# Layer 1 of a Strassen expert stage with tokens on the partitions: 512 moving columns, the gate in the relu, h turned by two DMAs a unit

## The chip, the cores and the metric

The kernel runs on one core of a Trainium2 chip. The metric is the device time of one execution in microseconds, taken as the median of several runs. Beside it stands one profiled execution, whose span (first to last instruction) all views of the profile divide up. The engines are PE (TensorE, with its weight loads as PEld), DVE (VectorE), ACT (ScalarE), POOL (GpSimd) and SP (SyncE, which here only issues DMAs).

## The reference

Attention with a sliding window of 128 and ALiBi bias on 8 batches, 8 heads, 576 positions and head size 64 gives x, 4608 tokens of 512 features. A dense mixture of 8 experts follows, with gates from a Sinkhorn iteration:

```python
logits = x @ w_gate
P = np.exp(logits - logits.max())
for _ in range(8):
    P /= P.sum(1, keepdims=True) + 1e-09
    P /= P.sum(0, keepdims=True) + 1e-09
    P *= N / E
for e in range(E):                     # E = 8, F = 1024, D = 512
    h = np.maximum(x @ w1[e], 0.0)
    out += P[:, e:e + 1] * (h @ w2[e])
```

Every token goes through every expert. P is positive, so P * relu(x @ w1) is relu((P x) @ w1) and also relu scaled after the fact.

## The kernel before

Attention comes first, batch by batch. Experts 0 and 1 are computed in the gaps of attention and of the gate iteration by a "filler": a list of small pieces (layer 1 with 512 token columns, layer 2 with 512 output columns) from which the program takes as many as the moment holds. Their results go to DRAM (ysp); x itself goes there too (xd).

From about 320 us on runs the stage that the change is about: experts 2 to 7 by Strassen's method in Winograd's form. The tokens are taken in 18 groups of 256 (two blocks of 128), and a **unit** is one group with one expert, 108 in all, in the order of the list `units`. Only the units of experts 6 and 7 in the first group use ordinary layer 1 matmuls (`l1_bank`), and the last unit an ordinary layer 2 (`plain`).

Layer 1 of a unit. x (scaled by the gate) lies in xset with the features on the partitions, cut into four quarters B11 to B22 and four sums T1 to T4 that DVE makes (`sums_x`, L947). Seven **parts** (`part`, L1014), named a11, s1, s2, a12, s3, s4, a22 after the quarter or sum of W1 that they use, are multiplied. Each part is four row blocks times two halves of the contraction: eight matmuls with a 128x128 block of W1 as stationary operand and 128 token columns moving. The hidden features come out on the partitions. The products are added up in three banks A, B and C of PSUM with the help of copies: after a11 ACT copies A to B; after s1 it copies C to s5; after s2 it copies B to C. a12 is then added to A and relu gives slot 0 of h; s3 is added to B, DVE adds s5 (below: **p+**) and relu gives slot 3; s4 is added to C, DVE adds s5 (**c+**) and relu gives slot 1; a22 is added to B and relu gives slot 2. Each of these waits is a hand-over between PE, ACT and DVE.

Layer 2 of a unit runs one unit later, between the parts of the next. Its left operands are the slots of h and the sums that DVE makes of them at the start of the next unit (`make_sums`, L1035: three operations, of 1024, 1024 and 512 columns). Seven **products** (`product`, L1048) of four matmuls each, a 128x128 block of h as stationary operand and 256 columns of W2 or a sum of its quarters moving, are added up in PSUM over the six experts of a group. At a group's end DVE gathers the seven sums into acc (`gather`), adds the results of experts 0 and 1 (`begin`), and the rows are stored (`finish`).

What feeds a unit. ACT multiplies the group's two x tiles by the gate (`scale_x`, L923, two operations a unit, for the unit after next); SP then turns each by a transposing DMA of 128x512 (`turn_xs`, L935). The tokens are reloaded once a group (L918, on SP's queue), as are the results of experts 0 and 1 (`load_y`, L1066, on SP's queue) and the stores (`finish`, on SP's queue). W1 and W2 sums of the experts (`quads_w1`, `sums_of`) are DVE work too, taken from a list by `some` in the first units (`more_sums`, L1156).

All orders are written out by hand: the program text is the order in each engine's queue (the loop at L1163), and waits come from the data alone. PSUM has four banks for the parts (tag pmm) and four for the sums of the products.

Of the kernel before, what the change touches and what calls it, by code (L numbers as in the profile page):

```python
# [14 lines left out]
def kernel(  # L15
# [89 lines left out]
    def unit_atoms(e, b0, nb, pool, tag, bufs, finish):  # L105
# [5 lines left out]
        halves = 2 if e == 0 and b0 < RI else 1  # L111
# [140 lines left out]
    if True:  # L252
# [314 lines left out]
        first_y: list = []  # L567

        def keep(e, blk, ps):
            if blk < RI and e == 0:  # L570
                if not first_y:
                    first_y.append(per.tile([P, RI, HD], FP16, name="y_first", tag="a8", bufs=8))
                nc.vector.tensor_copy(out=first_y[0][:, blk, :], in_=ps)
                if blk == RI - 1:
                    nc.sync.dma_start(out=ysp[0, 0:RI].rearrange("m p d -> p m d"), in_=first_y[0])
                return
            store(2)
# [324 lines left out]
        N = len(units)  # L902
        HF = Fd // 2
        h: dict = {}
        Ms: dict = {}
# [4 lines left out]
        xtok = [acc.rearrange("p m d -> p (m d)").bitcast(FP16)[:, HD * i : HD * i + HD] for i in range(2)]  # L910
        xs = [xset[i // 2][:, 4 + 2 * (i % 2) : 6 + 2 * (i % 2), :].rearrange("p q n -> p (q n)") for i in range(4)]

        def strassen(n):
            return n >= E - 2 or units[n][1] < E - 2

        def load_x(g):
            for m in range(2):
                nc.sync.dma_start(out=xtok[m], in_=xd[2 * g + m])  # L918

        load_x(groups[0])  # L920
        balance(7)

        def scale_x(n):  # L923
            if n >= N:
                return
            g, e = units[n]
            for m in range(2):
                blk = 2 * g + m
                nc.scalar.mul(out=xs[2 * (n % 2) + m], in_=xtok[m], mul=P_sb[:, blk, e : e + 1])  # L929
            if e == E - 1 and n + 1 < N:  # L930
                if g == groups[0]:
                    xtok[:] = [per.tile([P, HD], FP16, name=f"xtok_{i}", tag="yo", bufs=YO) for i in range(2)]
                load_x(units[n + 1][0])

        def turn_xs(n):  # L935
            if n >= N:
                return
            for m in range(2):
                nc.sync.dma_start(
                    out=xset[n % 2][:, 2 * m : 2 * m + 2, :].rearrange("p q (d t) -> p (q d) t", t=P),  # L940
                    in_=xs[2 * (n % 2) + m],
                    transpose=True,
                )
# [3 lines left out]
        def sums_x(n):  # L947
            if n >= N or not strassen(n):
                return
            x = xset[n % 2]  # L950
# [4 lines left out]
        def quads_w1(e):  # L955
# [5 lines left out]
            elif e == E - 1:  # L961
                t = per.tile([P, 2, 2, HF], FP16, name=f"s_{e}", tag="xT", bufs=4)
                q.update(s1=t[:, 0], s2=t[:, 1])
                q["s3"] = [per.tile([P, HF], FP16, name=f"s3_{k}", tag="yo", bufs=YO) for k in range(2)]
# [5 lines left out]
            def one(to, a, b, op):  # L970
                if isinstance(q[to], list):
                    for k in range(2):
                        nc.vector.tensor_tensor(out=q[to][k], in0=q[a][:, k], in1=q[b][:, k], op=op)
# [13 lines left out]
        def new_h(n):  # L987
            h[n] = per.tile([P, 8, NF2, P], FP16, name=f"hs_{n}", tag="hT", bufs=2)

        def l1_bank(n, i):  # L990
            g, e = units[n]
            if i == 0:
                new_h(n)
            x = xset[n % 2][:, 0:4].rearrange("p q (d t) -> p (q d) t", t=P).rearrange("p (b d) t -> p d b t", b=2)
            ps = aps.tile([P, 2, HB], FP32, name=f"psh_{n}_{i}", tag="pmm", bufs=4)
            for f in range(2):
                ft = 2 * i + f
                for dt in range(NDT):
                    nc.tensor.matmul(  # L999
                        out=ps[:, f, :],  # L1000
                        lhsT=W1L[e][:, dt, P * ft : P * ft + P],
                        rhs=x[:, dt],
                        start=(f == 0 and dt == 0),
                        stop=(dt == NDT - 1),
                        skip_group_check=True,
                    )
            fh, j = 2 * (i // 2), 2 * (i % 2)
            nc.scalar.activation(
                out=h[n][:, fh : fh + 2, j : j + 2, :].rearrange("p t f k -> p f t k"),
                in_=ps.rearrange("p f (t k) -> p f t k", t=2),  # L1010
                func=AF.Relu,
            )

        def part(n, ps, w, x, start=False):  # L1014

            q = SL[units[n][1]][w]
            q = q if isinstance(q, list) else [q[:, k] for k in range(2)]
            for j in range(NF2):
                for k in range(2):
                    nc.tensor.matmul(  # L1020
                        out=ps[:, j, :],
                        lhsT=q[k][:, P * j : P * j + P],
                        rhs=xset[n % 2][:, x, P * k : P * k + P],
                        start=(start and j == 0 and k == 0),
                        stop=(k == 1),
                        skip_group_check=True,
                    )

        def bank(n, name):
            return aps.tile([P, NF2, P], FP32, name=f"ps{name}_{n}", tag="pmm", bufs=4)  # L1030

        def relu(n, slot, src):
            nc.scalar.activation(out=h[n][:, slot], in_=src, func=AF.Relu)  # L1033

        def make_sums(n):  # L1035
            t = h[n]
            nc.vector.tensor_tensor(out=t[:, 4:6], in0=t[:, 0:2], in1=t[:, 2:4], op=ALU.add)  # L1037
            nc.vector.tensor_tensor(out=t[:, 6:8], in0=t[:, 1:4:2], in1=t[:, 0:3:2], op=ALU.subtract)
            nc.vector.tensor_tensor(out=t[:, 1], in0=t[:, 0], in1=t[:, 3], op=ALU.add)

        LEFT = {3: 0, 4: 3, 5: 4, 2: 5, 6: 6, 7: 7, 1: 1}
        RIGHT = {1: "f1", 2: "q11", 3: "f3", 4: "f4", 5: "q22", 6: "f6", 7: "f7"}
        BANK = {3: (0, 0), 4: (0, 1), 5: (1, 0), 2: (1, 1), 6: (2, 0), 7: (2, 1), 1: (3, 0)}

        def ends(n):
            return n >= 0 and units[n][1] == (E - 2 if units[n][0] == groups[-1] else E - 1)

        def product(n, *which):  # L1048
            if n < 0:
                return  # L1050
            g, e = units[n]
            for m in which:
                bk, half = BANK[m]
                if bk not in Ms:
                    Ms[bk] = mps.tile([P, 2, 2 * P], FP32, name=f"psM_{bk}")
                for f in range(NF2):
                    nc.tensor.matmul(  # L1057
                        out=Ms[bk][:, half, :],
                        lhsT=h[n][:, LEFT[m], f, :],
                        rhs=W2L[e][RIGHT[m]][:, f, :],  # L1060
                        start=(e == 2 and f == 0 and half == 0),
                        stop=(ends(n) and f == NF2 - 1 and (half == 1 or m == 1)),
                        skip_group_check=True,
                    )
# [17 lines left out]
        def gather(g, *which):  # L1082
            q4 = acc.rearrange("p m (c n) -> p (m c) n", c=2)
            for m in which:
                bk, half = BANK[m]
                ps = Ms[bk][:, half, :]
                for lo, step, op in {
                    1: ((0, 3, ALU.add),),
                    2: ((2, 0, ALU.add), (3, 0, ALU.subtract)),
                    3: ((1, 2, ALU.add),),  # L1090
                    4: ((0, 2, ALU.subtract),),
                    5: ((0, 0, ALU.subtract), (1, 0, ALU.add)),
                    6: ((3, 0, ALU.add),),
                    7: ((0, 0, ALU.subtract),),
                }[m]:
                    if step:
                        a = q4[:, lo : lo + step + 1 : step, :]
                        p2 = ps.unsqueeze(1).to_broadcast([P, 2, HB])
                    else:
                        a, p2 = q4[:, lo, :], ps  # L1100
                    nc.vector.tensor_tensor(out=a, in0=a, in1=p2, op=op)  # L1101
# [184 lines left out]
```

## Time and profile before

| what | us |
|---|---|
| median of 3 runs (1001.0 to 1003.34) | 1001.36 |
| the profiled execution | 1001.61 |
| its span | 999.8 |
| 340 to 980 us: PE busy of 640 | 639.92 |
| 340 to 980 us: DVE busy of 640 | 512.60 |
| 340 to 980 us: ACT busy of 640 | 528.83 |
| landing of the 212 turns of x, median | 2.5 |

The chain of waits is followed back from the last instruction; each step says which engine's work released the next. Its granted TensorE clock is 1.0 throughout. In a group's row stand the tile written and the tile read, the shape, the count, the busy time and the mean duration of one in ns. A matmul's duration is longer than the pitch at which matmuls follow each other, since they are pipelined; the pitch is read from the start times. A DMA's landing is counted from its issue.

### The profile page before, as it was taken

How to read it: one execution, taken by the hardware profiler on the slowest of the kernel's cores; microseconds unless marked ns; L12 is line 12 of the kernel's file. 1: busy time of each engine (PE TensorE's matmuls, PEld its weight loads, DVE VectorE, ACT ScalarE, POOL GpSimd, SP SyncE). 2: the span in 40 equal slices, each digit the busy share in tenths (PEclk: the TensorE clock that was granted, in tenths of full speed). 3: DMA queues.
4: the chain of work that ended last, by engine and by line, in shares of the span. 5: the costliest groups of instructions: out<-in, count | busy, mean ns of one | idle time of the engine just before them, and what ended most of it. 6: DMA issues, size and time to landing. Idle time of an engine off the chain costs nothing.

```text
span 999.8 us, 28277 instructions
## 1 busy us (share of the span) xinstructions
PE 988.3 (99%) x11731; PEld 816.0 (82%) x11731; DVE 762.0 (76%) x1593; ACT 718.0 (72%) x1216; POOL 110.0 (11%) x202
## 2 busy tenths in 40 slices
PE   7999999999999999999999999999999999999998
PEld 5645665566545899999999999999999999999997
DVE  5737677665688989887887787787787787787787
ACT  7655545554435768888888888888888888888885
POOL 3314444354110000000000000000000000000000
PEclk9999999999999999999999999999999999999999
DMA  9998999989997324333333433333433433333371
GB/s 250 212 271 218 187 233 230 234 170 183 222 201 152 81 54 97 82 61 94 86 56 95 86 76 75 88 73 75 96 76 65 99 78 65 96 76 66 96 116 49
DMA packets 264978, 123.08 MB, mean 123 GB/s; under 512 B 204433, under 2 KB 255633, under 8 KB 264849
## 3 DMA queue, kind: packets, MB, share of 16 engines
q1 hardware_dynamic: 249152, 100.65, 45.4%
q0 software_dynamic: 15264, 20.46, 11.5%
q8 instruction: 92, 1.51, 0.6%
q14 instruction: 38, 0.30, 0.1%
q10 hardware_dynamic: 432, 0.16, 0.1%
HBM read 78.30 MB, written 23.59 MB: 102 GB/s over the span
## 4 chain that ended last, share of the span: by engine, by line
PE 91%; DVE 5%; ACT 2%; DMA 1%; issue 1%; DVEq 0%; ACTq 0%
PE psM L1057 31%; PE psB L1020 14%; PE psy L159 11%; PE psA L1020 9%; PE psC L1020 9%; PE psh L137 9%; PE psh L118 3%; PE psS L457 1%; PE psN L491 1%; DVE pt L468 1%; DMA k<-in_k_dram 1%; ACT pt L463 1%; PE psh L999 1%; DMA xset<-xs 1%; DVE xsb L502 1%
## 5 line engine op out<-in xcount | busy, mean ns | idle before, releaser
L1057 PEld LDWEIGHTS <-hs 128*128 128x128 f16 x2996 | 271.0, 98 | 22.4 <-DVE hs L1037 0.4
L1057 PE MATMUL psM<-w2l,hs 128*128 128x256 f16 x1440 | 186.6, 273 | 0.2 <-DVE hs L1037 0.2
L1020 PEld LDWEIGHTS <-w1l 128*128 128x128 f16 x2848 | 181.4, 98 | 4.8 <-issue 0.4
L1033 ACT ACTIVATE hs<-hs 128x512 f16<-128x512 f16 x212 | 130.4, 629 | 36.2 <-DVE hs L1203 26.6
L1203 DVE TENSOR_TENSOR hs<-psB,s5y 128x512 f16<-128x512 f32 x106 | 73.3, 692 | 97.9 <-ACT xs L929 92.2
L1020 PEld LDWEIGHTS <-s 128*128 128x128 f16 x2136 | 141.6, 98 | 6.7 <-issue 0.2
L929 ACT ACTIVATE xs<-xtok,L_sb 128x512 f16<-128x512 f16 x204 | 135.8, 720 | 2.1 <-DMA xset<-xs 2.1
L159 PE MATMUL psy<-w2t,hT 128*128 128x512 f16 x576 | 135.3, 379 | 0.0
L1057 PE MATMUL psM<-more,hs 128*128 128x256 f16 x864 | 129.5, 273 | 0.0
L1020 PE MATMUL psB<-xset,s 128*128 128x128 f16 x1424 | 108.5, 219 | 0.1
L1020 PE MATMUL psA<-xset,w1l 128*128 128x128 f16 x1424 | 108.5, 219 | 0.0
L149 ACT ACTIVATE hT<-psh 128x512 f16<-128x512 f32 (+1 forms) x104 | 60.1, 581 | 63.5 <-PE psh L137 63.4
L159 PEld LDWEIGHTS <-hT 128*128 128x128 f16 x576 | 54.0, 98 | 58.2 <-issue 1.1
L463 ACT ACTIVATE pt<-psS 128x1024 f16<-128x1024 f32 x64 | 64.6, 1022 | 50.4 <-PE psS L457 49.9
L137 PE MATMUL psh<-xT,w1t 128*128 128x512 f16 (+1 forms) x448 | 99.0, 364 | 0.0
L1037 DVE TENSOR_TENSOR hs<-hs 128x1024 f16<-128x1024 f16 x107 | 73.9, 691 | 20.6 <-ACT hs L1033 18.6
L1194 ACT COPY psC<-psB 128x512 f32<-128x512 f32 x106 | 60.4, 570 | 38.6 <-PE psB L1020 38.6
L579 DVE CAST yo<-psy 128x512 f16<-128x512 f32 x65 | 44.6, 690 | 50.8 <-PE psy L159 50.1
L1186 ACT COPY s5y<-psC 128x512 f32<-128x512 f32 x106 | 62.2, 587 | 22.4 <-PE psC L1020 22.4
L615 POOL DMA_DIRECT2D w2t<-in_moe_w_dram x2 | 1.8, 882 | 669.0 <-PE psA L1020 661.0
L468 DVE TENSOR_TENSOR pt<-pt,mask 128x1024 f16<-128x1024 f16 x64 | 53.6, 837 | 28.3 <-ACT pt L463 28.1
L1101 DVE TENSOR_TENSOR acc<-acc,psM 128x256 f32<-128x256 f32 (+1 forms) x162 | 73.9, 503 | 0.3
(131 smaller groups left out, 1548.8 us busy)
## 6 DMA issues: line engine op xcount, KB each, us to landing
s5y<-ysp SPq DMA_DIRECT2D x36, 256.0 KB, 3.0
ysp<-yo SPq DMA_DIRECT2D x65, 128.0 KB, 4.4
v<-in_v_dram SPq DMA_DIRECT2D x32, 256.0 KB, 4.6
out_dram<-acc SPq DMA_DIRECT2D x31, 256.0 KB, 2.5
q<-in_q_dram SPq DMA_DIRECT2D x5, 1024.0 KB, 6.4
k<-in_k_dram SPq DMA_DIRECT2D x5, 1024.0 KB, 9.2
xtok<-xd SPq DMA_DIRECT2D x34, 128.0 KB, 2.3
w2t<-in_moe_w_dram POOLq DMA_DIRECT2D x4, 1024.0 KB, 12.3
```

What stands on the lines that cost most here:

```text
L137: nc.tensor.matmul(out=ps[:, 0:nt], lhsT=w1ts[e][:, dt, P * ft : P * ft + P], rhs=xT[:, at : at + nb, dt, :], start=(dt == 0), stop=(dt == ...
L159: nc.tensor.matmul(out=ps, lhsT=st["hT"][:, ft, P * ms : P * ms + P], rhs=w2ts[e][:, ft, :], start=(ft == 0), stop=(ft == NFT - 1),)
L463: nc.scalar.activation(out=pt, in_=ps.rearrange("p a y n -> p (a y) n"), func=AF.Exp, scale=scale)
L468: nc.vector.tensor_tensor(out=pt, in0=pt, in1=mask_of[kb][:, 4 * u : 4 * u + 4, :], op=ALU.mult)
L929: nc.scalar.mul(out=xs[2 * (n % 2) + m], in_=xtok[m], mul=P_sb[:, blk, e : e + 1])
L1020: nc.tensor.matmul(out=ps[:, j, :], lhsT=q[k][:, P * j : P * j + P], rhs=xset[n % 2][:, x, P * k : P * k + P], start=(start and j == 0 and ...
L1033: nc.scalar.activation(out=h[n][:, slot], in_=src, func=AF.Relu)
L1037: nc.vector.tensor_tensor(out=t[:, 4:6], in0=t[:, 0:2], in1=t[:, 2:4], op=ALU.add)
L1057: nc.tensor.matmul(out=Ms[bk][:, half, :], lhsT=h[n][:, LEFT[m], f, :], rhs=W2L[e][RIGHT[m]][:, f, :], start=(e == 2 and f == 0 and half = ...
L1101: nc.vector.tensor_tensor(out=a, in0=a, in1=p2, op=op)
L1186: nc.scalar.copy(out=s5, in_=pc)
L1203: nc.vector.tensor_tensor(out=h[n][:, 3], in0=pb, in1=s5, op=ALU.add)
```

## The change

Layer 1 of the stage is turned round: the x blocks become the stationary operand (two weight loads of 128x128 a part) and W1 moves, 512 columns at a time, so a part is two matmuls and the tokens come out on the partitions.

```diff
-        def part(n, ps, w, x, start=False):
-            for j in range(NF2):
-                for k in range(2):
-                    nc.tensor.matmul(
-                        out=ps[:, j, :],
-                        lhsT=q[k][:, P * j : P * j + P],
-                        rhs=xset[n % 2][:, x, P * k : P * k + P],
...
+        def part(n, name, w, x, start=False):
+            for k in range(2):
+                nc.tensor.matmul(
+                    out=psum(name),
+                    lhsT=xset[n // NE % 2][:, x, P * k : P * k + P],
+                    rhs=q[k],
...
```

x is no longer scaled: the gate, now one number per partition, is the scale of the relu. So x is turned and its sums are made once a group (`turn_x2`, `sums_x`, tokens XT0, XT1, SX), not once a unit. The relu writes hr, and h reaches the layout of layer 2 by two transposing DMAs of 128x1024 a unit, on SP's queue: the first after slots 0 and 3, the second after slots 1 and 2.

```diff
+        def relu(n, slot, src):
+            blk = 2 * g + slot % 2
+            nc.scalar.activation(out=hr[:, AT[slot]], in_=src, func=AF.Relu, scale=P_sb[:, blk, e : e + 1])
+
+        def turn_h(n, i):
...
+            nc.sync.dma_start(
+                out=hs[n % 2][:, 2 * i : 2 * i + 2].rearrange("p s f k -> p (s f) k"),
+                in_=hr[:, 2 * i : 2 * i + 2].rearrange("p s f -> p (s f)"),
+                transpose=True,
             )
+        def add_h(n, slot, name):
+            to = hr[:, AT[slot]]
+            nc.vector.tensor_tensor(out=to, in0=psum(name), in1=s5, op=ALU.add)
+            relu(n, slot, to)
+            if slot == 3:
+                turn_h(n, 0)
```

hr is one buffer, hs is two. The sums of h become five operations of 512 columns (`sum_h`, tokens t1, t4, t5, t6, t7). The products come in the order 3, 4, 2, 6, 1, 5, 7 from one stream over all units, and run one unit and four products behind: a unit does the last four of the unit before last and the first three (3, 4 and 2; the last of them needs t5) of the one before. Their sums rotate over five banks, four as before and one of pmm's; A, B and C are the other three. The order of a unit is a string of tokens, X being a product, W one weight sum, F a piece of the filler, g a gather:

```diff
+        plans = (
+            "a11 X s1 X s2 a12 X s3 p+ s4 c+ t5 X t6 t7 X X t4 a22 X t1",
+            "a11 g4 X s1 X g3 s2 g6 X g5 a12 s3 p+ s4 X c+ X X a22 t5 g7 t6 X t4 t1 t7 Y0 XL0",
+            "a11 g2 s1 X g1 FIN X s2 a12 X s3 p+ s4 X c+ X t5 t4 a22 XT0 t6 X X t7 t1 XL1",
+            "a11 X s1 X s2 a12 X s3 p+ s4 c+ X X t5 t6 a22 X XT1 t4 t1 t7 X B0 Y1",
+            "a11 X s1 X s2 a12 X s3 s4 p+ X c+ t5 X a22 X t4 t6 t1 X SX t7",
+            "a11 s1 X X s2 a12 X s3 s4 p+ X c+ X t5 t4 t6 a22 t7 t1 X X B1",
+        )
+        first = {
+            0: "a11 s1 W W F s2 a12 F W W s3 p+ s4 c+ F W W a22 F",
+            1: "a11 s1 F s2 a12 F s3 p+ s4 c+ t5 t6 X t1 X t4 a22 X t7 Y0",
+            4: "L0 X X L3 X X L1 t5 X t6 t4 X L2 X SX t7 t1",
+            5: "L0 X X L3 X X L1 t5 X t6 t4 X L2 X B1 t7 t1",
+            N - 1: "a11 s1 X B1 s2 X a12 X s3 p+ s4 X c+ t5 X t6 X a22 X t1 t4 g3 X t7 X g4 X g2 X g6 g1 g5 g7",
+        }
+        sums_at = {1: 3, 2: 3, 3: 2, 4: 4, 5: 3, 6: 3, 9: 4, 10: 3}
```

The loads of x (XL) and of experts 0 and 1 (Y) and the stores (FIN) move from SP's to POOL's queue; x has one token tile, so its second load waits until the first turn has read it:

```diff
         def load_y(g, e):
-            nc.sync.dma_start(out=y, in_=ysp[e, 2 * g : 2 * g + 2].rearrange("m p d -> p m d"))
+            nc.gpsimd.dma_start(out=y, in_=ysp[e, 2 * g : 2 * g + 2].rearrange("m p d -> p m d"))
...
-                    nc.sync.dma_start(out=out[t0 : t0 + P, :], in_=a)
+                    nc.gpsimd.dma_start(out=out[t0 : t0 + P, :], in_=a)
...
+                elif tok in ("XL0", "XL1"):
+                    if gi + 1 < len(groups):
+                        nc.gpsimd.dma_start(out=xst[int(tok[2])], in_=xd[2 * groups[gi + 1] + int(tok[2])])
```

Expert 7's weights are loaded earlier, within the gate iteration, as soon as expert 0's last result is kept; three of its W1 sums lie in six tiles of another tag. Its W2 is reloaded for the last unit in eight pieces over four units, not in one piece. The last block of expert 1 has layer 2 pieces of half the size, and six of them (not three whole ones) are left for the stage's first units. The two halves of the last unit's layer 2 start with the features whose transpose comes first.

```diff
         for it in range(7):
             balance(it)
-        aux = per.tile([P, 4, NF2, HB], FP16, name="aux", tag="w2t", bufs=2)
+            if first_done and E - 1 not in W1L:
+                load_last(E - 1)
...
-        while filler.l1 or filler.todo or len(filler.l2) > 3:
+        while filler.l1 or filler.todo or len(filler.l2) > 6:
...
-            if n == N - E + 2:
-                load_w2(E - 1)
+            if N - NE + 1 <= n < N - 1:
+                for i in range(2):
+                    load_w2(E - 1, 2 * (n - N + NE - 1) + i, 8)
```

More of the change, by code (lines that the diff above doesn't have):

```diff
@@ L109, in unit_atoms @@
         st: dict = {}
-        halves = 2 if e == 0 and b0 < RI else 1
+        halves = 2 if (e == 0 and b0 < RI) or (e == 1 and b0 == NBLK - 4) else 1
         def l1_pair(ft):
@@ L576, in keep @@
                 return
+            if e == 0 and blk == NBLK - 1:
+                first_done.append(blk)
             store(2)
@@ L1029, in bank @@
[L1029 to L1048, printed above, removed]
+        pp: dict = {}
+        def psum(name):
+            if name not in pp:
+                pp[name] = aps.tile([P, GT], FP32, name=f"ps{name}", tag="pmm", bufs=4)
+            return pp[name]
@@ new lines, in part @@
+        def part(n, name, w, x, start=False):
+            g, e = units[n]
+            q = SL[e][w]
+            q = q if isinstance(q, list) else [q[:, k] for k in range(2)]
+            for k in range(2):
[3 more added lines that the diff above has]
+                    rhs=q[k],
+                    start=(start and k == 0),
+                    stop=(k == 1),
+                    skip_group_check=True,
+                )
@@ new lines, in plain_l1 @@
+        def plain_l1(n, slot, name):
+            g, e = units[n]
+            m, fh = slot % 2, slot // 2
+            for dt in range(NDT):
+                nc.tensor.matmul(
+                    out=psum(name),
+                    lhsT=xset[n // NE % 2][:, 2 * m + dt // 2, P * (dt % 2) : P * (dt % 2) + P],
+                    rhs=W1L[e][:, dt, HF * fh : HF * fh + HF],
+                    start=(dt == 0),
+                    stop=(dt == NDT - 1),
+                )
+            relu(n, slot, psum(name))
@@ L1049, in product, with sum_h @@
+        def add_h(n, slot, name):
[4 more added lines that the diff above has]
+                turn_h(n, 0)
+        def sum_h(n, to):
             if n < 0:
                 return
-            g, e = units[n]
[L1052 to L1064, printed above, removed]
+            t = hs[n % 2]
+            x, y, op = {
+                5: (1, 3, ALU.add),
+                6: (1, 0, ALU.subtract),
+                1: (0, 3, ALU.add),
+                4: (0, 2, ALU.add),
+                7: (3, 2, ALU.subtract),
+            }[to]
+            nc.vector.tensor_tensor(out=t[:, AT.get(to, to)], in0=t[:, AT[x]], in1=t[:, AT[y]], op=op)
@@ new lines, in ends, with product @@
+        def ends(n):
+            return units[n][1] == (E - 2 if units[n][0] == groups[-1] else E - 1)
+        stream = [(n, m) for n in range(N - 1) for m in ORDER]
+        def product():
+            n, m = stream.pop(0)
+            g, e = units[n]
+            half = BANK[m][1]
+            ps = sum_of(g, m)
+            for f in range(NF2):
+                nc.tensor.matmul(
+                    out=ps,
+                    lhsT=hs[n % 2][:, LEFT[m], f, :],
+                    rhs=W2L[e][RIGHT[m]][:, f, :],
+                    start=(e == 2 and f == 0 and half == 0),
+                    stop=(ends(n) and f == NF2 - 1 and (half == 1 or m == 1)),
+                    skip_group_check=True,
+                )
```

331 lines of the change are left out of this document (139 added, 192 removed).

## The prediction

> **What bounds the kernel now.** I read the page first (busy shares, then the chain of waits), then the chain between 623 and 642 us, then the timeline of one unit, then the DMA answers.
>
> ```profile
> span 999.8 us, 28277 instructions
> PE 988.3 (99%) x11731; PEld 816.0 (82%) x11731; DVE 762.0 (76%) x1593; ACT 718.0 (72%) x1216; POOL 110.0 (11%) x202
> PE 91%; DVE 5%; ACT 2%; DMA 1%; issue 1%; DVEq 0%; ACTq 0%
> ```
>
> PE sets the end, and from 340 to 980 us nothing else does. So the question is how fast PE issues, and whether it will wait. The chain shows the pitch of its groups (start, length, group):
>
> ```profile
> 623.39 0.45 PE psA L1020 x8
> 623.84 0.87 PE psM L1057 x8
> ...
> 629.57 0.45 PE psA L1020 x8
> ...
> 635.76 0.45 PE psA L1020 x8
> ```
>
> A unit takes (635.76 - 623.39)/2 = 6.185 us. Its seven products (28 matmuls of 256 columns) are seven times 0.87/2 = 0.436, together 3.05. That leaves 3.13 for the seven layer 1 parts: 0.448 each, eight matmuls of 128 columns. What 512 columns cost is seen in the chain of the earlier stage:
>
> ```profile
> 308.65 1.74 PE psy L159 x8
> 310.39 1.73 PE psh L137 x8
> ```
>
> Eight in 1.73 to 1.74 us: 0.216 each.
>
> **The change, part by part.**
>
> *Pitch.* 106 of the 108 units use the seven parts; a part becomes two matmuls of 512 columns: 2 x 0.216 = 0.4325 to 0.435 for 0.448. Seven times 0.013 to 0.0155 is 0.09 to 0.108 us a unit, times 106: 9.6 to 11.5. I take **-11.0**. It is small because the columns streamed stay the same (56 x 128 = 14 x 512). The new unit has 3.03 + 3.05 = 6.08 us of PE work.
>
> *ACT and DVE.* Scaling x (two ACT ops at 0.665 pitch, 1.33 us a unit) goes; four relus gain a scale per partition, at most the 0.05 by which the scaling's pitch exceeds the relu's (1.33/2 against 1.23/2). ACT falls from 5.1 to some 4 us a unit. DVE saves five of six x sums (0.42 + 0.29 + 0.29) and makes five h sums of 0.425 for 0.69 + 0.69 + 0.43: 0.5 less a unit on the whole. Both lie beside 6.08 us of PE and cost nothing unless a hand-over is late.
>
> *Hand-overs.* In the timeline of one unit (start, length, what, idle before):
>
> ```profile
> 703.16 0.61 PE L1020 MATMUL psB<-xset,s 128*128 128x128 f16 x8
> 703.61 0.61 PE L1020 MATMUL psA<-xset,w1l 128*128 128x128 f16 x8
> 703.87 0.57 ACT L1194 COPY psC<-psB 128x512 f32<-128x512 f32 x1 [0.35 <-PE psB L1020]
> ```
>
> ACT starts 0.26 after PE's next group (703.61) begins. At 974.84 a copy of 0.58 us ends at 975.42 and PE, which waited, goes on at 975.47, so 0.05 back. Part s3 needs the copy C<-B made after s2: 0.26 + 0.57 + 0.05 = 0.88 us. Before, a part and two products lay between (0.45 + 0.87); now a part and one product, 0.868. Short by 0.012, times 106: **+1.3** (0 to 4). All other copies keep over 0.3 us of slack.
>
> *The turning of h.* Two transposes of 128x1024 a unit for two of 128x512. The two answers that bound them (128x512, then 128x2048; issue time, then landing):
>
> ```profile
> L939 SPq DMA_TRANSPOSE xset<-xs x117: 1188/1192/2415, 600.5 to 959.1; - x117
> DMA to landing us min/median/max: 2.4/2.5/4.7
> ...
> L332 SPq DMA_TRANSPOSE qk<-c x10: 1852/2526/3972, 80.1 to 208.6; - x10
> DMA to landing us min/median/max: 4.4/5.3/7.1
> ```
>
> A third of the way between the minima: issue 1.19 + 0.22 = 1.41, landing 2.4 + 0.67 = 3.1 (bounds 2.5 and 5.3). I take 3.1, since the stage's DMA share is 0.38 and qk ran at 0.8. SP spends 2.8 us of 6.08 on it; stores and the loads of y leave its queue for POOL's. With unit time 0 at a11: s3 ends at 3.47, DVE's add p+ runs 3.73 to 4.42, relu to 5.16, first transpose issued 5.19 to 6.61. c+ ends at 5.01, its relu 5.79, the last relu 6.42; second transpose issued at 6.67, which is 0.59 of the next unit, landing at 3.69. Who waits: c+ of the next unit (it overwrites what is being turned), due at 4.33, and behind it on DVE sum t5, due to end at 5.36, needed by the seventh product at 5.64. So c+ may start at 4.56: **slack 0.87 us**. The first transpose lands at 2.2 and is wanted (by a relu) at 3.0.
>
> *Late transposes.* The stage has some that land late:
>
> ```profile
> DMA to landing us min/median/max: 2.4/3.3/4.2
> ...
> q8 instruction: 10, 0.16, 0.7%
> ```
>
> The first line is the pair at 631.4 and 632.7 us: 2.4 and 4.2. Of the 208 I asked for singly, 153 landed within 3.2, 26 within 3.3 to 3.9, 29 at 4.0 or later. That comes, I infer, from the fetching of instructions: 10 transfers of 16 KB in 100 us, 0.7% of 16 engines, so one engine held for 1.1 us every 10 us, while a transpose needs all. PE's instructions fall from 168 to 84 a unit, so half as many fetches; but a transfer twice as wide is exposed longer. By this, of 106 second transposes 7 to 14 are about 1.05 late and 4 to 7 about 1.7 late; over the slack that is 0.2 and 0.85: 4 to 9. Bounds: 0 (slack covers all) to 17 (55 of 208 is 26%; 26% of 106 is 28, by 0.6 each). I take **+5**, as a shorter issue would lengthen the slack.
>
> *The end.* The last unit keeps four more products (moved work, no cost), but its second layer now waits for a transpose: last relu at 6.5, landing 6.7 + 3.1 = 9.8; PE gets there at 7.83 + 0.86 = 8.7. Stall 1.1 to 1.6, against 0.2 before (991.72, PE idle 0.20 behind DVE): **+1.2** (0 to 2.5).
>
> *The start of the stage.* psA starts at 328.90 and 335.71, a unit of 6.81: 0.63 lost, since DVE makes weight sums and h sums in the unit that needs them, and 0.15 at 366.6. The products now come some four later and the sums are spread: **-0.8** (-1 to +2).
>
> *Moved DMAs.* x, y and the result go by POOL, each with over 6 us before it is needed. POOL's own 128 KB stores (xd<-xsb) landed at a median of 3.2 us, so I put this at 0. [...]
>
> Sum: -11.0 + 1.3 + 5 + 1.2 - 0.8 = **-4.3**. The profiled execution took 1001.61, 1.8 of it outside the span: 997.3; the median (1001.36) is 0.25 lower: **997**.
>
> **Rivals.** (1) *The transposes are never late beyond the slack*: without +5, 992. For: the slack is 0.87 and half as many fetches. Against: 29 of 208 landed 1.6 late or more. (2) *Late ones at the upper bound*: +17 for +5, 1009; between, 1001 to 1009. (3) *The transpose sets the pace*, the slow side: landing L, c+ 0.05 after it, t5 ready and a product started 1.08 later, 0.49 to the unit's end, and the issue at 0.48 of the next: the unit is L + 2.1. It decides from L = 3.95, and the kernel is slower from L = 4.1; at the 4.4 of the 128x2048 row 6.5 us, +0.32 x 106: 1035. For: loops of this kind repeat in every unit. Against: half the width, half the DMA load. (4) *No gain of pitch* (512 columns between 256-column groups cost what eight of 128 do): 1008. Against: 1.73 in either neighbour in the earlier stage. (5) *POOL's transfers come late*: the second x transpose stands in SP's queue before the next h. At the 11.6 us of POOL's w1l row an x load misses its 8 us by 3.5, and h comes 1.5 to 3 late in 17 groups: 1022 to 1047. [...]
>
> **How the numbers follow.** Forecast 0.54 (own range 992 to 1000.5), rival 1 0.14, 2 0.11, 3 0.13, 4 0.05, 5 0.03. A difference within 0.3% (998.4 to 1004.4) can't be told from none. Below it lie 0.40 of the forecast and rival 1: 0.54. Within it 0.14 of the forecast, 0.04 of rival 2, 0.01 of 4: 0.19. Above, the rest: 0.27. The range 988 to 1009 leaves out rivals 3 and 5 and little else.
>
> **What would show it.** Right: units of 6.09 to 6.12 us in the chain, most with no wait of PE; hr transposes landing near 3.1; a few waits of PE's products on DVE's h sums of 0.2 to 1 us, at fetches. Wrong: landings over 4 in most units; a wait in every unit before s3 over 0.05; SP waiting for an x load; two 512-column matmuls taking over 0.44.

## The result, and the profile after

The changed kernel is slower: 1014.37 us (median of 5 runs, 1012.94 to 1016.18) against 1002.88 (1001.0 to 1003.78, 5 runs) for the kernel before, a ratio of 1.0119 with a 95% interval of 1.0102 to 1.0137. The prediction was 997, with a range of 988 to 1009. The profiled execution took 1014.62, 13.0 more than that of before.

The page of the changed kernel: the span, busy times, the instruction queue, and the chain by engine and by line.

```profile
span 1012.8 us, 19357 instructions
PE 985.9 (97%) x7247; PEld 624.6 (62%) x7247; DVE 685.7 (68%) x1546; ACT 626.4 (62%) x1000; POOL 181.0 (18%) x317
q8 instruction: 57, 0.93, 0.4%
PE 81%; DMA 11%; DVE 5%; ACT 1%; issue 1%; DVEq 0%; ACTq 0%
PE psM L1071 27%; PE psy L159 12%; PE psB L983 11%; DMA hs<-hr 10%; PE psh L137 9%; PE psA L983 8%; PE psC L983 7%; PE psh L118 3%; DVE hr L1027 2%; PE psS L457 1%; PE psN L491 1%; DMA k<-in_k_dram 1%; DVE hs L1043 1%; DVE pt L468 1%; ACT pt L463 1%
```

PE is busy for 2.4 us less than before in a span 13.0 longer, so it waits. The wait has a name: DMA has gone from 1% of the chain to 11%, nearly all of it hs<-hr, the turning of h. The chain between 598 and 640 us shows how (start, length, what):

```profile
600.62 0.31 PE psA L983 x2
600.93 4.78 DMA hs<-hr
...
605.80 0.69 DVE hr L1027
606.50 0.34 DVE hs L1043
...
607.49 0.43 PE psA L983 x2
...
613.58 0.43 PE psA L983 x2
...
619.66 0.29 PE psA L983 x2
619.95 4.79 DMA hs<-hr
```

The rows of psA that open a unit stand at 600.62, 607.49, 613.58, 619.66: one unit of 6.87 us, then two of 6.09 and 6.08. The short ones are what the sum said (6.08 of PE work, and no wait at s3). In the long one a transpose, issued at 600.93, lands after 4.78 us; c+ (L1027) and t5 (L1043) run behind it, as the prediction had them, and PE's seventh product starts 0.8 us late. The same happens at 619.95, 19.0 us later, which is three units and one wait. All turns of h between 400 and 960 us land like this:

```profile
L1019 SPq DMA_TRANSPOSE hs<-hr x181: 1232/1238/1457, 399.1 to 960.0; - x181
...
DMA to landing us min/median/max: 3.0/3.2/5.2
```

Issue 1.24 (1.41 foreseen) and landing 3.2 (3.1 foreseen): the usual transpose is as predicted. The late ones decide.

What fell late with them is in the DMA answer for the single microsecond from 603 to 604:

```profile
q8 instruction: 1, 0.02, 5.5%
```

One fetch of instructions, one packet of 16 KB (0.93 MB in 57 on the page): 5.5% of 16 engines for 1 us is 0.88 us of one engine. The page above counts 57 such fetches for 7247 matmuls and as many weight loads, 254 to a fetch. The page of the kernel before, with 11731 of each, has

```profile
q8 instruction: 92, 1.51, 0.6%
```

which is 255 to a fetch. I take it from the two that these are PE's instructions. With the waits on semaphores that PE also has (137 in the changed kernel's trace, 34 in that of before) it is 257 and 255, so I put a fetch at some 256 of them, an estimate from these counts. A unit has 84 matmuls and weight loads, so by this estimate three units hold almost exactly one fetch, and it comes back to the same place in every third unit. Read from the trace, fetch by fetch:

```
units from      fetch, us after the unit's start   waits of PE
376 to 530 us   1.5 to 2.4                         14, of 0.2 to 0.4, in 8 of 9 such units
546 to 835 us   3.0 to 3.5                         12, of 0.7 to 1.2, in 12 of 16 such units
849 to 960 us   4.0 to 4.7                         none
```

The waits add up to 14.3 us between 378 and 850 us; in the kernel before, PE had none there. A wait is taken here from the start times, as the time by which a matmul starts later than the pitch; the idle time in the profile's rows runs from a matmul's modelled end and is some 0.16 us less for each.

The end of the stage is the other place. The chain from 994 us on:

```profile
994.22 6.37 DMA hs<-hr
...
1001.76 3.85 PE psM L1071 x20
1005.61 1.90 PE psA L1133 x8
```

The last five products, twenty matmuls and 2.2 us at the usual pitch, take 3.85 us. The table by stretches of 1 us (busy time of each engine with its number of instructions, then the granted clock, the DMA share and GB/s) says why:

```profile
1001.00:1002.00 1.00, 0.24 (x3) 0.22 (x4) 1.00 (x3) 0.60 (x1) 0.00 (x0) 1.00 1.06 205
1002.00:1003.00 1.00, 1.00 (x9) 0.83 (x7) 0.97 (x4) 0.70 (x2) 0.00 (x0) 0.71 0.30 55
1003.00:1004.00 1.00, 1.00 (x7) 0.69 (x5) 1.00 (x3) 0.00 (x0) 0.00 (x0) 0.50 0.06 12
...
1005.00:1006.00 1.00, 1.00 (x5) 0.54 (x4) 0.86 (x3) 0.00 (x0) 0.00 (x0) 0.58 0.21 40
1006.00:1007.00 1.00, 1.00 (x6) 0.47 (x5) 0.90 (x3) 0.00 (x0) 0.00 (x0) 1.00 0.00 0
```

After a pause of 2.2 us PE runs at half its clock for some 3.4 us, which costs 1.6.

So the 13.0 us divide, by the waits of PE in the two traces:

| what | us |
|---|---|
| pitch: 106 x (6.185 - 6.085) | -10.6 |
| waits from 378 to 850 us (none before) | +14.3 |
| start of the stage, to 370 us: 2.9 against 0.8 | +2.1 |
| after 960 us: waits of 4.8 against 0.6 | +4.2 |
| the half clock at the end | +1.6 |
| attention, code not touched, by 213 us: differs from run to run | +1.1 |
| not placed | +0.3 |

The first 2687 matmuls are the same in all thirteen kernels, and the last of these starts between 320.3 and 324.0 us, so the 1.1 us of attention say nothing about the change.

### The profile page after: what moved, and what is told of

Same layout as the page of the kernel before. It is cut to its first block, busy times and chain, and to the rows that moved or that the text cites. A ratio compares the mean times of both kernels' runs of the same rounds, so it can differ in the third digit from the quotient of the medians.

```text
span 1012.8 us, 19357 instructions
## 1 busy us (share of the span) xinstructions
PE 985.9 (97%) x7247; PEld 624.6 (62%) x7247; DVE 685.7 (68%) x1546; ACT 626.4 (62%) x1000; POOL 181.0 (18%) x317
## 4 chain that ended last, share of the span: by engine, by line
PE 81%; DMA 11%; DVE 5%; ACT 1%; issue 1%; DVEq 0%; ACTq 0%
PE psM L1071 27%; PE psy L159 12%; PE psB L983 11%; DMA hs<-hr 10%; PE psh L137 9%; PE psA L983 8%; PE psC L983 7%; PE psh L118 3%; DVE hr L1027 2%; PE psS L457 1%; PE psN L491 1%; DMA k<-in_k_dram 1%; DVE hs L1043 1%; DVE pt L468 1%; ACT pt L463 1%
## 5 line engine op out<-in xcount | busy, mean ns | idle before, releaser
L1071 PEld LDWEIGHTS <-hs 128*128 128x128 f16 x2996 | 291.2, 98 | 160.9 <-DVE hs L1043 20.6
L1013 ACT ACTIVATE hr<-hr,L_sb 128x512 f16<-128x512 f16 x212 | 144.2, 716 | 92.7 <-DVE hr L1027 90.7
L1027 DVE TENSOR_TENSOR hr<-psB,s5y 128x512 f16<-128x512 f32 x106 | 73.3, 692 | 184.2 <-PE psB L983 141.2
L1043 DVE TENSOR_TENSOR hs<-hs 128x512 f16<-128x512 f16 x535 | 192.7, 418 | 1.1 <-DMA hs<-hr 0.4
L983 PEld LDWEIGHTS <-xset 128*128 128x128 f16 x1484 | 144.5, 97 | 76.2 <-issue 4.0
L983 PE MATMUL psA<-w1l,xset 128*128 128x512 f16 x356 | 105.9, 379 | 0.4 <-ACT hr L1013 0.4
L983 PE MATMUL psB<-s,xset 128*128 128x512 f16 x356 | 105.6, 378 | 0.0
L1013 ACT ACTIVATE hr<-psA,L_sb 128x512 f16<-128x512 f32 x110 | 76.0, 691 | 26.3 <-DMA hs<-hr 18.3
L1027 DVE TENSOR_TENSOR hr<-psC,s5y 128x512 f16<-128x512 f32 x106 | 72.5, 683 | 16.4 <-DMA hs<-hr 12.3
L1180 ACT COPY psB<-psA 128x512 f32<-128x512 f32 x106 | 60.4, 570 | 33.5 <-PE psA L983 33.5
L1013 ACT ACTIVATE hr<-psB,L_sb 128x512 f16<-128x512 f32 x108 | 72.7, 673 | 2.9 <-PE psB L996 1.1
```

The source lines that it names most:

```text
L983: nc.tensor.matmul(out=psum(name), lhsT=xset[n // NE % 2][:, x, P * k : P * k + P], rhs=q[k], start=(start and k == 0), stop=(k == 1), ski ...
L1013: nc.scalar.activation(out=hr[:, AT[slot]], in_=src, func=AF.Relu, scale=P_sb[:, blk, e : e + 1])
L1027: nc.vector.tensor_tensor(out=to, in0=psum(name), in1=s5, op=ALU.add)
L1043: nc.vector.tensor_tensor(out=t[:, AT.get(to, to)], in0=t[:, AT[x]], in1=t[:, AT[y]], op=op)
L1071: nc.tensor.matmul(out=ps, lhsT=hs[n % 2][:, LEFT[m], f, :], rhs=W2L[e][RIGHT[m]][:, f, :], start=(e == 2 and f == 0 and half == 0), stop= ...
L1180: nc.scalar.copy(out=psum("B"), in_=psum("A"))
```

## The experiments

Four runs were compared on one chip, beside one set of runs of the kernel before (1003.23); four on another (1003.13), two on a third (1002.99) and one on a fourth (1002.33). All ratios are to the kernel before on the same chip. First the waits in the middle of the stage: are they the fetches, other traffic, or a loop that sets its own pace?

**One product later.** Unit 1, the second of each group and the last unit place one product later, which carries on into all units. The first product that needs t5 of the unit before then stands behind the next a11, which is 0.87 us more slack (a product and a part).

```diff
-            1: "a11 s1 F s2 a12 F s3 p+ s4 c+ t5 t6 X t1 X t4 a22 X t7 Y0",
+            1: "a11 s1 F s2 a12 F s3 p+ s4 c+ t5 t6 t1 X t4 a22 X t7 Y0",
...
-            "a11 g4 X s1 X g3 s2 g6 X g5 a12 s3 p+ s4 X c+ X X a22 t5 g7 t6 X t4 t1 t7 Y0 XL0",
+            "a11 g4 X s1 X g3 s2 g6 X a12 s3 p+ s4 X c+ X X a22 t5 g5 t6 X g7 t4 t1 t7 Y0 XL0",
...
```

> The products run one more product behind: a unit does the last five of the unit before last and only products 3 and 4 of the one before, so nothing in a unit needs t5 of the unit before. Theory 'fetch' (an instruction fetch for PE holds one DMA engine for about 1 us, the second transpose of h in every third unit lands 1.6 us late, and the 0.87 us of slack are too few): the slack becomes 0.87 + 0.436 + 0.432 = 1.74 us, the waits of every third unit (13 to 14 us between 380 and 850 us) vanish but for 0.1 each, the end loses 1 to 3 us of its 5: 997 to 1002. Rival 'traffic' (the transfers of POOL at fixed places of a group make the transpose late): the same, since the lateness is covered too. Rival 'pace' (the chain landing, c+, relu, relu, transpose is as long as the unit): less than 3 us gained, 1011 or more.

1003.43 us, ratio 0.9995 (0.9984 to 1.0006), just above the 997 to 1002 that I had put. A loop that sets the pace (rival 3 of the prediction) would have kept its time; it falls. The waits between 378 and 960 us shrink to 16, of 0.14 to 0.28, 3.6 us in all. Most of them (13) are now at s2, which waits for ACT's copy of A to B behind the relus that came late. Fetches and other traffic are not told apart by this.

**The fetch moved.** 29 matmuls of 512 columns in units 2 to 5 are cut into two of 256. The work is the same; 58 more PE instructions shift the place of every later fetch.

```diff
+        splits = [29]
+        def wide(n, out, lhsT, rhs, start, stop):
+            if 2 <= n <= 5 and splits[0] > 0:
+                splits[0] -= 1
+                cuts = ((0, GT // 2), (GT // 2, GT))
...
```

> 29 matmuls of 512 columns in units 2 to 5 are each done as two of 256 columns, 58 more PE instructions, after which the program is as before. Cost of the split itself 29 x 0.0025 = 0.1 us. Theory 'fetch': instructions are fetched 256 at a time, three units have nearly 256, so the fetch falls at the same place of every third unit; 58 instructions move it from instruction 24 to 45 of a unit (1.6 to 3.4 us after its start) to 50 to 75 (4 to 6 us), where no transpose is hurt: the waits between 380 and 960 us vanish, 13 to 14 us gained, 1000 to 1002. Rivals 'traffic' and 'pace': nothing moves, 1014 within 2.

1000.23 us, ratio 0.9966 (0.995 to 0.9982): below the kernel before. The chain of 600 to 640 us by line, of the changed kernel and of this one:

```profile
by line: DMA hs<-hr 35.7%; PE psM L1071 34.7%; PE psB L983 13.6%; PE psA L983 10.9%; PE psC L983 8.6%; DVE hr L1027 3.5%; DVE hs L1043 1.7%; issue 0.6%; DVEq L1027 0.1%
```

```profile
by line: PE psM L1083 51.1%; PE psB L986 21.7%; PE psC L986 14.0%; PE psA L986 13.5%
```

The transposes are gone from it. The fetch is not: in the microsecond from 614 to 615 stands

```profile
q8 instruction: 1, 0.02, 6.4%
```

1.02 us of one engine, but in a unit that opened at 609.38, so 5 us in. The second transpose, in flight from some 0.4 to 3.5 us of the next unit (607.85 to 610.98, where the unit opened at 607.49, in the changed kernel's trace), has landed by then, and the first of this unit is issued only at 614.42, 0.07 us before the fetch begins; it lands after 3.0 us. In this run all fetches from 376 to 944 us come 4.0 to 5.7 us after the unit's start, and PE has two waits over 0.12 us in all of 378 to 960 (0.16 and 0.13). The stores, the loads and the lengths of DVE's and ACT's work are those of the changed kernel, so other traffic and the pace both fall as causes. In the changed kernel's trace it can be counted turn by turn: of its 185 turns of h between 378 and 955 us, 31 had a fetch that began 1.0 to 3.1 us after their issue, and 27 of these landed after 4.0 us or more (median 4.7); of the other 154, 6 did (median 3.2).

**The fetch moved by one whole unit.** The control, as an edit of the run before: 42 cuts are the 84 instructions of a unit, so the fetch should hit the same place one unit earlier.

```diff
-        splits = [29]
+        splits = [42]
```

> As the run before, but 42 matmuls are split: 84 instructions, the number of one unit. Theory 'fetch': the fetch falls at the same place as in the changed kernel, but one unit earlier (units with n mod 3 = 2 instead of 0): the waits stay as many, 1014 within 3, and stand in other units. 'Traffic': the waits stay where they are (n mod 3 = 0), 1014. It also shows that splitting alone gains nothing.

1017.72 us, ratio 1.0124 (1.0104 to 1.0144), which can't be told from the changed kernel's 1.0119. The fetches stand in the units before those of the changed kernel (the 5th, 8th, 11th of the list and not the 6th, 9th, 12th), 1.65 to 2.5 us and later 3.0 to 3.5 us after their start, and the waits have moved with them: 26, of 17.5 us. That cutting matmuls helps by itself is out too. The time is 0.7 us above the 1014 within 3 that I had put: all 16 fetches from 524 to 811 us cost a wait, not 12 of 16.

**A part as eight matmuls of 128 columns.** With four matmuls for each of the two, the instructions per unit are again 168, with everything else as in the changed kernel.

```diff
+                for j in range(NF2):
+                    nc.tensor.matmul(
+                        out=psum(name)[:, P * j : P * j + P],
+                        lhsT=xset[n // NE % 2][:, x, P * k : P * k + P],
+                        rhs=q[k][:, P * j : P * j + P],
...
```

> Each of a part's two 512-column matmuls is done as four of 128 columns with the same stationary block; all else as in the changed kernel. The pitch term of the prediction: a unit without waits goes from 6.085 back to 6.18, +10 us. Theory 'fetch': 168 PE instructions a unit, a fetch every one and a half units, so about twice the waits, +10 to +17: together 1033 to 1042. 'Traffic': the pitch alone, 1024.

1030.0 us, ratio 1.025 (1.0223 to 1.0277). Units without a wait take 6.18 us, so the term of the pitch is confirmed to 0.005 us a unit: +10 us for 128 columns. The waits rise from 14.3 to 20.6 us between 378 and 960, which is neither as many as twice the fetches would give nor as few as unchanged traffic. The places tell: up to 570 us one of the two fetches in every three units falls 1.7 to 3.4 us after a unit's start and mostly costs a wait, the other at 4.1 to 5.7 us and hardly ever does; later both drift, and still mostly one of the two costs a wait. The 1030.0 lies between the two theories (1024, and 1033 to 1042). I had counted fetches where their places had to be read.

Then the ends of the stage.

**No reload of expert 7's W2.** Its eight pieces go to POOL's queue in pairs, at 968.07, 978.14, 990.32 and 991.39, near the issue of transposes of h (967.74, 979.42, 992.89, 994.22), and these land after 4.9, 5.8, 5.3 and 6.4 us. Here the two overwritten quarters are got back by subtraction.

```diff
-            if N - NE + 1 <= n < N - 1:
-                for i in range(2):
-                    load_w2(E - 1, 2 * (n - N + NE - 1) + i, 8)
+            if n in (N - 4, N - 3):
+                q = W2L[E - 1]
+                to, a = (("q12", "q11"), ("q21", "q22"))[n - N + 4]
+                nc.vector.tensor_tensor(out=q[to], in0=q[to], in1=q[a], op=ALU.subtract)
```

> The changed kernel, without the reload of expert 7's W2: the two quarters that were overwritten (by f6 = q11 + q12 and f7 = q21 + q22) are got back by two subtractions on VectorE in units N-4 and N-3. It is still the reference's computation. Theory (the 1 MB of the reload, issued by POOL at 968 to 992 us, makes transposes of h late at the end): of the 4.8 us that PE waits after 960 us, 1.06 at 972.5 and 0.66 + 0.38 + 0.25 at 984 to 987 go, 2.0 to 2.4 in all, and the pause before the end stays (its cause is the last transpose and a fetch at 998.5): 0.998 of the changed kernel, 1012 to 1012.9 where before is 1002.9. Rival (these are late by instruction fetches, as in the stage before): within 0.5 us of the changed kernel, 1014.

1009.82 us, ratio 1.0065 (1.0045 to 1.0084): more than either theory gave. The pause at 999.4, which I had put down to a fetch, is gone as well, though the fetch stays (at 997.5, when the transposes before it have landed). The last chain:

```profile
998.66 0.45 PE psB L983 x2
...
999.85 3.13 DMA hs<-hr
...
1003.02 1.04 PE psA L1133 x4
```

PE runs without a wait until the last relu's transpose lands; after 960 us it waits 1.1 us in all, and the granted clock is 1.00 to the end. So the reload costs some 5 us: 4 of late transposes, and the half clock after the pause that the longest of them brings.

**The reload in one piece.** Is it the eight pieces, or the 1 MB? First at the place where the kernel before has it:

```diff
-            if N - NE + 1 <= n < N - 1:
-                for i in range(2):
-                    load_w2(E - 1, 2 * (n - N + NE - 1) + i, 8)
+            if n == N - E + 2:
+                load_w2(E - 1)
```

> The changed kernel, with expert 7's W2 reloaded in one transfer of 1 MB issued behind unit N-6, as in the kernel before, not in eight pieces over four units. Theory (it is the spreading that costs: each pair of pieces makes another transpose of h late, five units in all, and the last of them makes the pause and the drop of the clock): one transfer, landed in some 10 us, spoils two units at most and is over 20 us before the end: waits of PE after 960 us of 1 to 2 us and no drop of the clock, 1010 to 1011.5 where before is 1003. Rival (any reload of 1 MB beside these transposes costs the same): 1013 to 1015.

1021.87 us, ratio 1.0188 (1.0165 to 1.021), and no test: in the changed order four products of unit N-7 stand behind this place, so they waited for the reload (PE idle for 10.9 us from 966.9) and read the new quarters. One unit later it can be compared:

```diff
-            if n == N - E + 2:
+            if n == N - NE + 1:
```

> As the run before it, but with the one transfer of 1 MB issued a unit later, behind unit N-5, where no product still reads the old quarters (in the run before, four products of unit N-7 that stood behind it in the program waited 10.9 us for it and read the new values). The two theories are as they were. Spreading costs: waits of PE after 960 us of 1 to 2.5 us, no drop of the clock, 1010 to 1011.5 where before is 1003. Any reload of 1 MB beside these transposes costs the same: 1013 to 1015.

1019.96 us, ratio 1.0175 (1.0141 to 1.021): both theories fall, the whole transfer is worse than its pieces. From the chain, and the table by stretches behind the wait:

```profile
972.44 13.13 DMA hs<-hr
```

```profile
984.00:985.00 1.00, 0.00 (x0) 0.00 (x0) 0.00 (x0) 0.00 (x0) 0.00 (x0) 0.50 1.06 346
...
988.00:989.00 1.00, 1.00 (x6) 0.70 (x5) 0.84 (x3) 0.50 (x1) 0.00 (x0) 0.50 0.66 132
989.00:990.00 1.00, 1.00 (x9) 0.70 (x7) 0.00 (x0) 0.01 (x1) 0.00 (x0) 0.99 0.92 176
```

A transpose that is in flight beside 1 MB lands after 13.1 us, PE idles for 8.0, and the clock is at 0.50 until 989. The cost comes with the transfer beside the transposes and not with the spreading: in one piece it was higher than in eight, and without the reload it was gone.

**The last chains cut in half.** Added to the run without the reload: the matmuls that need only the first transpose of the last h come first in all three banks.

```diff
...
-        plain(1, "A", 0, HD)
-        plain(0, "C", 0, HB)
-        plain(0, "B", HB, HD)
+        for part_ in range(2):
+            plain(1, "A", 0, HD, part_)
+            plain(0, "C", 0, HB, part_)
+            plain(0, "B", HB, HD, part_)
```

> The kernel without the reload, and with the last unit's three ordinary layer 2 chains cut in half: first the halves that need only the first transpose (16 matmuls, 1.7 us), then the others. Theory: the pause of 2.2 us at 999.4 falls under 0.9, and the granted clock, which was at 0.5 for some 3 us after that pause, stays near 1.0 to the end: 2.5 to 3.5 us less than the kernel without the reload alone, 1009 to 1010 where before is 1002.9. Rival (the drop of the clock at the end has another cause than the pause): only 1.3 to 1.6 us less than the kernel without the reload, and the clock falls as before.

1010.42 us, ratio 1.0068 (1.0045 to 1.0091), not to be told from the run without the reload. The 2.5 to 3.5 us that were to be gained on that run are not there; that the number lies near 1009 to 1010 is luck, as the pause that the edit was to shorten was gone already. (The halves that come first are 12 matmuls, not 16.) It saves the second of the last two waits (0.62 and 0.32) at most. The clock stays at 1.00, as it did without the reload alone, so the run decides nothing on the pause.

**The start.** Two edits: weight sums behind p+ and c+ in unit 0, and the last slot of the two ordinary units in bank B.

```diff
-            0: "a11 s1 W W F s2 a12 F W W s3 p+ s4 c+ F W W a22 F",
+            0: "a11 s1 W W F s2 a12 F s3 p+ s4 c+ F a22 W W F W W",
...
-                    plain_l1(n, slot, {0: "A", 3: "B", 1: "C", 2: "A"}[slot])
+                    plain_l1(n, slot, {0: "A", 3: "B", 1: "C", 2: "B"}[slot])
```

What they aim at, in the changed kernel's timeline of DVE and then of PE:

```profile
325.31 0.69 DVE L582 CAST yo_last<-psy 128x512 f16<-128x512 f32 x1 [0.74 <-PE psy L159]
325.92 0.68 DVE L958 TENSOR_TENSOR s<-s,w1l 128x1024 f16<-128x1024 f16 x1
326.63 0.69 DVE L958 TENSOR_TENSOR w1l<-w1l,s 128x1024 f16<-128x1024 f16 x1
327.25 0.68 DVE L1027 TENSOR_TENSOR hr<-psB,s5y 128x512 f16<-128x512 f32 x1
```

```profile
327.98 0.59 PE L983 MATMUL psB<-w1l,xset 128*128 128x512 f16 x2 [0.98 <-DVE hr L1027]
```

p+ (327.25) stands behind a cast and two weight sums, and a22 waits for it.

> The changed kernel with two edits at the start of the stage: in unit 0 the third pair of weight sums and the one before it stand behind p+ and c+, not ahead of them, and the last slot of the two ordinary units goes to bank B, not A. Theory (PE waits 1.15 us for p+ behind weight sums at 326.6, and 0.57 + 0.56 for a bank that ACT's relu still reads at 354.5 and 361.5): 2.0 to 2.3 us less than the changed kernel, about 1012 where before is 1002.9. Rival (the waits only move on to the next unit, whose sums come later): less than 0.7 us gained.

1013.41 us, ratio 1.0102 (1.0078 to 1.0125); the intervals of this ratio and the changed kernel's overlap. In the traces PE's waits to 370 us fall from 2.9 to 1.4 us: the three aimed at (1.15, 0.57, 0.56) are gone, but 0.7 us comes back in unit 1 (332 us), whose p+ and sums are later now, and 0.43 at 354.4. It lies between the two theories.

**All of it.** The 29 cuts, the start, no reload and the halved chains together; then the same with the products one place later as well.

> All of it together: the changed kernel with 29 matmuls of 512 columns split in units 2 to 5 (the fetches then fall 4 to 5.7 us into every third unit), the edits at the start, no reload of W2, and the last chains cut in half. If the four causes add: 1000.2 (the split alone) less 2.2 at the start, less 2 to 2.4 for the reload and 1.5 to 3 for the end: 993 to 995, 0.991 of the kernel before. If they hide behind each other (DVE or ACT become the bound once PE no longer waits): 997 or more.

> The kernel with all four edits, and the products one place later as well, as in the run that had only that. If waits of PE that a longer slack can take up are left (about 2.5 us of 6.0: those at 356 us, at 904 and at 983), 993 to 994.5 where before is 1003; if the later products bring waits of their own (they brought 0.2 to 0.3 us in 16 units when they stood alone), as much or more than the 995.4 of the kernel without it.

995.37 us, ratio 0.9919 (0.99 to 0.9939), and 994.28 us, ratio 0.9909 (0.9892 to 0.9927). The first lies between what was put for causes that add (993 to 995) and for causes that hide (997 or more), nearer to the first. Added up, the gains of the 29 cuts, of the start and of the run with the halved chains over the changed kernel give a ratio of 0.990, within the interval of 0.9919: so the causes add as far as these runs can tell. The later products make no difference beyond the intervals. Both beat both kernels, by some 8 and 9 us against before. The page of the first:

```profile
span 994.1 us, 19403 instructions
PE 979.3 (99%) x7276; PEld 628.4 (63%) x7276; DVE 683.8 (69%) x1548; ACT 623.3 (63%) x1000; POOL 176.5 (18%) x309
```

PE is at 99% again, as in the kernel before, with 9.0 us less work.

## Why the prediction was wrong

The forecast was 4.3 us faster, and the profiled execution is 13.0 slower. Of these 17.3 us the late transposes make 9.3, the end 4.6 and the start 2.9.

*The pitch* was right: -11.0 foreseen, -10.6 measured, and the run with 128 columns gave it back. Rival 4 falls.

*The hand-over* from s2 to s3 costs nothing (1.3 foreseen, 0 to 4): units without a late transpose take 6.08 us, the bare work. The 0.012 us by which it was short was less than the reading of the rows could carry.

*The turning of h* was right in landing (3.1 for 3.2), in slack (0.87; a turn 1.6 us late makes PE wait 0.8, so 0.8 were there) and in who waits; its issue is shorter (1.24 for 1.41). The loop doesn't set the pace; rival 3 falls, and so does rival 1, by which no turn was late beyond the slack.

*The late transposes* were the step that failed: +5 for a measured +14.3, within its bounds of 0 to 17. The cause was named (a fetch; a transpose beside one lands after 4.8 us, not 3.2), and the number of units hit was right too: 20 with a wait in the changed kernel, 11 to 21 foreseen. What was wrong is that I treated the collisions as chance. I took the shares of late transposes of the kernel before, as if a fetch fell anywhere. With 84 instructions a unit and some 256 a fetch it falls at nearly the same place in every third unit, for hundreds of us. So there were 12 large waits (4 to 7 foreseen), of 0.85 us on average as foreseen, 10.2 us together; and the other 8 units lost 0.5 us each (0.2 foreseen), in six of them by a pair of waits. By the same count it could have been nothing: with 58 more instructions ahead of them two waits over 0.12 us are left, of 0.16 and 0.13. It was to be read from the diff, 28 instructions for the parts and 56 for the products, times three, and from the 92 fetches of the kernel before.

*The end* was the second: +1.2 (0 to 2.5) for a measured +4.2 and another +1.6 of half clock. The stall behind the last relu was about what the step said (1.1 us remain without the reload). What the step lacked is the reload of W2 in eight pieces, which stood in the diff and which I priced nowhere. In the kernel before, the reload of 1 MB at 961.8 also made transposes late (two turns of x landed after 6.8 and 5.8 us), but PE waited only 0.6 us after 960 us: nothing needed them so soon.

*The start* was -0.8 (-1 to +2) for a measured +2.1. I had counted on later products and spread sums; but a cast and two weight sums stand ahead of p+ in unit 0 (1.15 us), and the two ordinary units use one bank twice running (0.56 each). The order was there to read.

*The moved DMAs* cost nothing that shows, as said: the loads of y land at a median of 3.3 us (3.0 on SP's queue before), those of x at 2.7 (2.3 before), and with the same loads and stores the run with 29 cuts has next to no waits between 378 and 960 us. Rival 5 falls.

Rival 2 (late ones at the upper bound, 1009) was the nearest; the start and the end of the stage made most of the rest to 1014.4.

## What to carry to other kernels

Where a transposing DMA like these (3.2 us to landing, 4.8 beside a fetch) stands on the path, work out how many instructions a loop iteration has and how that stands to the size of a fetch (84 and some 256 here): if a few iterations together hold a whole number of fetches, the collision is not a chance but a place, and it can be moved by a few instructions (58 here: 1014.37 to 1000.23 us) or covered by slack (0.87 us more: 1003.43). Count every transfer in the diff that shares the time with such a DMA, also those that the path doesn't wait for: beside 1 MB in pieces these landed after 4.9 to 6.4 us. And look for the wait ahead of the end: what looked like the last unit's cost was a transfer issued units before.

## What was not expected of the hardware

A fetch is one packet of 16 KB that takes some 0.9 to 1.0 us (0.88 and 1.02 in the rows above; the 32 between 376 and 960 us of the changed kernel have a median of 0.96), but a transpose in flight beside it lands 1.6 us late (4.8 for 3.2). While only one transpose was moving, from 607.2 to 607.6 us, the DMA share was 1.11, with 14 to 21 of its packets under way at once; that it needs all 16 engines is what I conclude from this. The packets show a part of the rest. Of the late transpose issued at 600.93 the last data move at 603.6, and of its last 32 packets, of 4 bytes each, 30 start at 603.29 to 603.56; the other two start at 604.51 and 604.52, at the end of the fetch (603.64 to 604.52). It lands 1.2 us after them, where a usual one lands 0.5 us after its last packet (median of the 154). Why these 0.7 us come on top of the fetch stays open.

A pause of PE of 2.2 us was followed by a clock of 0.50 for 3.4 us; so were 2.1 us in the run with the edits at the start and 1.8 us in the run with the products later. The 1.5 us before 988.4 in the run with the 29 cuts were not: the clock there is 1.00 from 984 to 992. In the changed kernel the fall came at 1002.42 us, 0.66 after PE had gone on (1001.76), and the clock was back at 1.00 at 1005.83. How long a pause has to be for a fall is not shown.
